# Weight halves of a block-causal attention and two-FFN kernel: four early ones held back to the last pair, two loads begun ahead, a new pace and new ranks

## The chip, the cores and the metric

The kernel runs on one core of one Trainium2 chip. The metric is the device time of one execution in microseconds (us), the median of several runs; lower is better. Five engines work side by side, each through its own queue in order: TensorE (PE in the profile), VectorE (DVE), ScalarE (ACT), GpSimd (POOL) and SyncE (SP), which here only issues DMA loads and stores.

## The reference

```python
scores = scale * np.matmul(q, k.transpose(0, 1, 3, 2))      # 4 batches, 8 heads, 576 x 64
scores = np.where(block_i >= block_j, scores, -1000000000.0)  # blocks of 64 rows
scores = scores - np.max(scores, axis=-1, keepdims=True)
attn = np.exp(scores)
attn = attn / (np.sum(attn, axis=-1, keepdims=True) + 1e-09)
...
x = np.ascontiguousarray(attn_out.transpose(0, 2, 1, 3)).reshape(B * S, H * D)  # 2304 x 512
h = x @ w_in                    # 512 x 2048
x = (np.maximum(h, 0.0) ** 2) @ w_out
h = x @ w_in2                   # 512 x 2048
return (h * np.cos(h)) @ w_out2
```

All of it is float32.

## The kernel before

The kernel has two parts: attention, up to about 200 us, and the two feed-forward layers after it.

**Attention** handles heads two at a time, in 16 pairs (0 to 15). For each pair TensorE makes the scores of nine row blocks (L374; block i has 64 (i + 1) columns, and the ninth, of 576, goes to the tile `wide`), VectorE takes each block's maximum (L386, tile `nmax`), ScalarE the exponential with its sum (L391, tile `P`), GpSimd adds the small constant to the sums (L416), VectorE inverts them (L422) and GpSimd scales `P` (L431). TensorE then transposes `P` in seven groups (L452). ScalarE copies the result as the high part of a two-part float (L457, `PTh`), and VectorE subtracts it for the low part (L460, `PTl`). GpSimd splits the values into two parts likewise (L486, L492, `vhl`), and TensorE makes the weighted sums (L517), once for each head and each of two column ranges. ScalarE moves half of such a sum across partitions (L528, `half`); VectorE joins it for the first head (L531), and ScalarE (L534) with GpSimd (L537) for the second. A pair of the first four, when done, is a quarter of the input of the first layer's block 0; the "cut" splits it in two parts (ScalarE L315, VectorE L318, tiles `xs`).

What stands in which engine's queue during attention is decided by a planner (`Plan.emit`): a list scheduler that takes on each engine the step that can begin first by its own planned costs, and of several the one with the lowest rank (`RANK`, plus ten for each pair). Only the resulting order reaches the chip.

**Weights.** Each weight matrix of a layer comes in 32 halves (chunk c of 16; h = 0 for the first matrix, 1 for the second), stored so that each half has to be converted to a high and a low float before TensorE can use it. A half is loaded (L202, four `raw` buffers) and then takes six VectorE instructions (L205 shift, L212 mask, L223 join, L235 sign, L241 power, L265 the low part, tile `w`), two ScalarE instructions (L218 rebias, L229 fraction), and one that writes the high part: on GpSimd during attention (L259), on ScalarE in the layers (L256). The order of use is c0h0, c1h0, c2h0, c0h1, c3h0, c1h1, c4h0, c2h1 and so on; I number them 0 to 31. The first `EARLY = 6` (0 to 5) are converted within attention, at whatever place the planner finds.

**The layers.** The rest is converted in `convert()`, called between the steps of block 0: one call finishes the half in `begun` and begins the next. A block is 512 (sometimes 256 or 384) rows; a step is one chunk c. Step s emits the hidden product of chunk s (12 matmuls, L624), then the pending work of earlier steps (L646, L647 and L636 on ScalarE for step s - 1; the low part L639 on VectorE for step s - 2), then the calls of `convert()`, as many as `PACE` has saved up, then the output product of chunk s - 3 (12 matmuls, L688). In its last step a block also emits the four cuts of the next block's input (L315, L318).

Of the kernel before, what the change touches and what calls it, by code (L numbers as in the profile page):

```python
# [24 lines left out]


RANK = {
    "load": -128.3,
    "k scale": 45.0,
    "scores": 2.3,  # L30
    "maximum": -18.9,
    "exponential": 254.4,
    "guard": -115.1,
    "invert": -17.2,
    "scale": 54.0,
    "turn": 14.8,
    "turned high": -66.6,
    "turned low": -5.4,
    "value load": -0.0,
    "value high": -10.0,  # L40
    "value low": 64.2,
    "weighted": 20.6,
    "move": 282.2,
    "join": -71.6,
    "keep": 114.2,
    "add": 147.2,
    "zeros": 429.5,
    "weights": 403.5,
    "cut": 1000000.0,
}  # L50

# [79 lines left out]
def tile_block_causal_attention__then__two_ffn(  # L131
# [13 lines left out]
    NPAIR, _, S = kT.shape  # L145
    D = vp.shape[4]
# [23 lines left out]
    nc.vector.memset(new_bias, -7.0 * 2.0**30)  # L170

    WARM = 15
    EARLY = 6
    NA = 5
    w_a = ctx.enter_context(tc.tile_pool(name="w_a", bufs=NA))
    xs_p = ctx.enter_context(tc.tile_pool(name="xs", bufs=1))
# [8 lines left out]
    weights = {}  # L185
    LAG = 3
    loads = [((layer, c), h) for layer in range(2) for c in range(KF) for h in range(2)]
    loads.sort(key=lambda x: (x[0][0], x[0][1] + LAG * x[1], -x[1]))
    loads.reverse()
    loaded, begun = [], []  # L190
# [81 lines left out]
    def flush():  # L272
        while later:
            later.pop()()

    def convert():

        old = new = None
        flush()
        if begun:  # L280
            (layer, c), h = begun[0].key, begun[0].h
            if layer == 1 and c >= freed[h]:
                return
            old = begun.pop()
            old.sign()
        if loaded:
            new = loaded.pop()
            begun.append(new)
            new.shift()
        if old:  # L290
            old.power()
            old.high()
        if new:
            new.mask()
            new.rebias()
        if old:
            old.low()
        if new:
            new.join()
            later.append(new.fraction)  # L300
        if loads:
            loaded.append(Half(*loads.pop()))
            loaded[0].load()

    class Cut:

# [18 lines left out]
    def attention():  # L325
        with ExitStack() as actx:
            ap = actx.enter_context(tc.tile_pool(name="ap", bufs=1))
            ps = actx.enter_context(tc.tile_pool(name="ps", bufs=1, space=PSUM))
            plan = Plan([ps.tile([128, 512], F32, name=f"ps{r}") for r in range(6)])
# [170 lines left out]
            def add_weighted(p, e, i0, i1):  # L500

                rank = 10 * p + e + i0 / 20
                b, hp = divmod(p, KD)
                mine, other = slice(e * D, (e + 1) * D), slice((1 - e) * D, (2 - e) * D)
                pt = [t.rearrange("p (s e d) -> p s e d", e=2, d=D) for t in PT]
                todo = [
                    (j, max(i0, 2 * j), x)
                    for j in range(NCH)
                    if 2 * j < i1
                    for x in range(1 if j == NCH - 1 else 2)  # L510
                ]
                w, at = (i1 - i0) * D, slice(i0 * D, i1 * D)

                def product(bank):
                    for n, (j, a, x) in enumerate(todo):
                        s0 = j_off[j] + a - 2 * j
                        nc.tensor.matmul(  # L517
                            bank[:, (a - i0) * D : w],
                            lhsT=vhl[:, j, e].rearrange("p x d -> p (x d)"),
                            rhs=pt[x][:, s0 : s0 + i1 - a, e, :],  # L520
                            start=(n == 0),
                            stop=(n == len(todo) - 1),
                        )

                x = xall[mine, hp, b * S : (b + 1) * S][:, at]

                def move(bank):
                    nc.scalar.activation(out=half[e][mine, at], in_=bank[other, 0:w], func=AF.Copy)  # L528

                def join(bank):  # L530
                    nc.vector.tensor_tensor(out=x, in0=bank[mine, 0:w], in1=half[e][mine, at], op=ALU.add)  # L531

                def keep(bank):
                    nc.scalar.activation(out=x, in_=bank[mine, 0:w], func=AF.Copy)  # L534

                def add():
                    nc.gpsimd.tensor_tensor(out=x, in0=x, in1=half[e][mine, at], op=ALU.add)  # L537

                need = sorted({n // 4 for n, (_, i) in enumerate(seq) if i0 <= i < i1})
                keys = [f"{x}{g}" for x in ("PTh", "PTl", "room") for g in need] + ["vh", "vl"]  # L540
                cost = sum(max(0.107, (i1 - a) * D / 2400 + 0.0135) for _, a, _ in todo)
                s = plan.add("P", cost, ("weighted", rank), product, keys, [f"O{p}.{e}.{i0}"], holds=1)
                product_, half_, x_ = f"O{p}.{e}.{i0}", f"half{e}.{i0}", f"x{b}.{hp}.{e}.{i0}"
                out_of = lambda f: lambda bank=None: f(plan.held[s][0])
                plan.add("A", 0.052 + w / 1200, ("move", rank), out_of(move), [product_], [half_])
                if e == 0:
                    plan.add("V", 0.07 + w / 960, ("join", rank), join, [product_, half_], [x_], frees=s)
                else:
                    plan.add("A", 0.052 + w / 1200, ("keep", rank), keep, [product_, half_], [x_], frees=s)
                    plan.add("G", 0.22 + w / 430, ("add", rank), add, [half_], [x_])  # L550

            def add_zeros(r):
# [8 lines left out]
            def add_half(n):  # L561
                x = Half(*loads.pop())
                raw, high, bits = f"raw{n % 4}", f"high{n % 4}", f"bits{n % 2}"
                rank = ("weights", n)
                plan.add("D", 2.0, rank, x.load, writes=[raw, high])
                plan.add("V", 0.34, rank, x.shift, writes=[raw])
                plan.add("V", 0.34, rank, x.mask, [high], [bits])
                plan.add("A", 0.61, rank, x.rebias, writes=[bits])
                plan.add("V", 0.6, rank, x.join, [high], [raw])
                plan.add("A", 0.52, rank, x.fraction, writes=[raw])  # L570
                plan.add("V", 0.6, rank, x.sign, [high], [bits])
                plan.add("V", 0.34, rank, x.power, [bits], [high])
                plan.add("G", 0.67, rank, x.high_beside, [bits])
                plan.add("V", 0.6, rank, x.low, [raw, high])
# [5 lines left out]
            for p in range(NPAIR):  # L580
# [10 lines left out]
                for e in range(2):  # L591
                    for i0, i1 in ((0, 4), (4, NB)):
                        add_weighted(p, e, i0, i1)
            for n in range(EARLY):
                add_half(n)
            for kk in range(KD):
                x = Cut(0, S // 128 * 128, kk)
                keys = [f"x0.{kk}.{e}.{i0}" for e in range(2) for i0 in (0, 4)]
                plan.add("A", 0.52, ("cut", kk), x.high, keys, [f"xs{kk}"])
                plan.add("V", 0.6, ("cut", kk), x.low, [f"xs{kk}"])  # L600
                first.append(x)
# [3 lines left out]
    def layers():  # L605
# [112 lines left out]
                t0 += n  # L718
        last = max(i for i, b in enumerate(blocks) if b[0] == 0)
        steps = [(i, c) for i in range(len(blocks)) for c in range(KF)]  # L720
        PACE = {0: 1.67, last: 1.75, last + 1: 0.75}
        owed = 0.0
        gss = {}
        xs = first
# [1 line left out]
        for step in range(len(steps) + LAG):  # L726
# [4 lines left out]
            if step < len(steps):  # L731
                i, c = steps[step]
                layer, t0, n = blocks[i]
                while (layer, c, 0) not in weights:
                    convert()
                gss[step], *fresh = hidden(layer, c, xs, n)
# [10 lines left out]
            if step < len(steps) and i == last:  # L747
                freed[0] = c + 1
            owed += PACE.get(i, 2)
            while owed >= 1:  # L750
                owed -= 1
                convert()
            if step >= LAG:
                i, c = steps[step - LAG]
                layer, t0, n = blocks[i]
                while (layer, c, 1) not in weights:
                    convert()
                output(layer, gss.pop(step - LAG), n, c)
                if i == last:
                    freed[1] = c + 1  # L760
                if c == KF - 1:
                    finish(layer, t0, n)

    with tc.manual_schedule():
        attention()
        layers()
# [43 lines left out]
```

## Time and profile before

| | |
|---|---|
| median of 3 runs | 1002.77 us (1002.02 to 1002.93) |
| the profiled execution | 1002.03 us, of which the profile spans 1000.2 |
| busy in the span | PE 981.9, DVE 625.4, ACT 591.7, POOL 175.3 us |
| mean granted TensorE clock | 0.997 |
| first hidden product | begins at 201.86 us |

Busy time of TensorE is modelled and says little in the attention part; what the other engines wait for, and where each engine is full in a stretch, says more. All times below are microseconds from the span's start, in one execution.

### The profile page before, as it was taken

The numbers are of one execution on the slowest core, as the hardware profiler recorded it, in microseconds if no ns is written. First come the engines' busy times: TensorE is split into PE (matmuls) and PEld (weight loads), VectorE is DVE, ScalarE is ACT, GpSimd is POOL, SyncE is SP. The second block draws the span as 40 slices with busy tenths as digits, with TensorE's granted clock in tenths as the row PEclk, the third lists the DMA queues.
The fourth block names the chain that finished last, engine by engine and source line by source line (L and its number), as shares of the span: only waits on it lengthen the run. The fifth ranks groups of instructions, "written<-read, shape, count | busy, mean of one in ns | idle before, by whom it ended". The sixth has DMA issues, their size and how long they took to land.

```text
span 1000.2 us, 13835 instructions
## 1 busy us (share of the span) xinstructions
PE 981.9 (98%) x4895; PEld 823.4 (82%) x4895; DVE 625.4 (63%) x1260; ACT 591.7 (59%) x1224; POOL 175.3 (18%) x292
## 2 busy tenths in 40 slices
PE   9999999999999999999999999999999999999998
PEld 7767788788678889988888888888888888899997
DVE  6899877779972121211169999966555655656554
ACT  7999899878873343443368886644334434434433
POOL 6999988800000000000000000000000000000000
PEclk9999999999999999999999999999999999999999
DMA  6442233235430000000014442001000100100000
GB/s 220 144 140 98 76 121 99 99 96 168 161 123 1 1 1 1 2 1 1 1 64 142 162 138 85 1 1 42 0 1 1 43 1 1 43 1 1 32 1 32
DMA packets 18806, 58.56 MB, mean 59 GB/s; under 512 B 1968, under 2 KB 2096, under 8 KB 18736
## 3 DMA queue, kind: packets, MB, share of 16 engines
q1 hardware_dynamic: 18736, 57.68, 17.3%
q8 instruction: 38, 0.62, 0.3%
q14 instruction: 32, 0.26, 0.1%
HBM read 52.95 MB, written 4.72 MB: 58 GB/s over the span
## 4 chain that ended last, share of the span: by engine, by line
PE 78%; DVE 11%; ACT 4%; POOL 4%; issue 2%; DMA 0%; SPq 0%; DVEq 0%; ACTq 0%; POOLq 0%
PE acc L688 36%; PE h L624 36%; DVE w L265 2%; POOL P L431 2%; PE ps L374 2%; PE ps L517 2%; ACT P L391 2%; DVE nmax L386 2%; PE ps L452 1%; DVE bits L235 1%; DVE raw L223 1%; DVE PTl L460 1%; ACT PTh L457 1%; DVE raw L241 1%; DVE gs L639 1%
## 5 line engine op out<-in xcount | busy, mean ns | idle before, releaser
L624 PE MATMUL h<-xs,w 128*128 128x512 f32 (+2 forms) x1920 | 422.1, 369 | 2.0 <-ACT w L256 1.5
L624 PEld LDWEIGHTS h<-xs,w 128*128 128x128 f32 x1920 | 344.1, 188 | 59.8 <-ACT w L256 3.6
L688 PE MATMUL acc<-gs,w 128*128 128x512 f32 (+1 forms) x960 | 210.2, 368 | 0.0
L688 PE MATMUL acc<-w,gs 128*128 128x512 f32 x864 | 209.7, 391 | 0.0
L688 PEld LDWEIGHTS acc<-gs,w 128*128 128x128 f32 x960 | 168.4, 189 | 29.9
L639 DVE TENSOR_TENSOR gs<-g,gs 128x512 fp32r<-128x512 f32 (+2 forms) x160 | 101.3, 634 | 141.6 <-ACT gs L636 141.5
L688 PEld LDWEIGHTS acc<-w,gs 128*128 128x128 f32 x864 | 161.9, 188 | 32.1
L636 ACT CAST gs<-g 128x512 fp32r<-128x512 f32 (+2 forms) x160 | 92.3, 577 | 149.9 <-DVE g L671 96.7
L657 DVE SCALAR_TENSOR_TENSOR g<-turns,h 128x512 f32<-128x512 int32 (+1 forms) x80 | 50.7, 634 | 123.0 <-ACT turns L654 122.2
L431 POOL TENSOR_SCALAR P<-P,rinv 128x64 f32<-128x64 f32 (+2 forms) x144 | 87.4, 624 | 5.9 <-DVE rinv L422 2.8
L654 ACT ACTIVATE turns<-h 128x512 int32<-128x512 f32 (+1 forms) x80 | 44.2, 552 | 70.5 <-PE h L624 70.4
L374 PE MATMUL ps<-kB,qB 128*128 128x64 f32 (+7 forms) x256 | 83.1, 425 | 1.2 <-DMA qB<-in_qd_dram 0.9
L646 ACT ACTIVATE g<-h 128x512 f32<-128x512 f32 (+1 forms) x80 | 43.8, 548 | 66.2 <-PE h L624 66.2
L452 PEld LDWEIGHTS ps<-ident,P 128*128 128x128 f32 (+1 forms) x400 | 47.4, 141 | 36.0 <-DVE PTl L460 11.0
L668 ACT ACTIVATE g<-g,half_pi 128x512 f32<-128x512 f32 (+1 forms) x80 | 54.6, 682 | 36.8 <-DVE g L662 36.8
L391 ACT ACTIVATE P<-ps,nmax 128x64 f32<-128x64 f32 (+7 forms) x128 | 64.4, 506 | 10.8 <-DVE nmax L386 9.3
L452 PE MATMUL ps<-ident,P 128*128 128x128 f32 (+1 forms) x400 | 63.6, 280 | 7.2 <-POOL P L431 3.1
L460 DVE TENSOR_TENSOR PTl<-ps,PTh 128x512 fp32r<-128x512 f32 x96 | 64.3, 683 | 7.2 <-ACT PTh L457 6.8
L386 DVE TENSOR_REDUCE nmax<-ps 128x1 f32<-128x64 f32 (+7 forms) x128 | 55.6, 444 | 10.7 <-PE ps L374 10.0
L517 PE MATMUL ps<-PTh,vhl 128*128 128x320 f32 (+3 forms) x224 | 59.7, 301 | 2.0 <-POOL vhl L492 1.5
L457 ACT CAST PTh<-ps 128x512 fp32r<-128x512 f32 (+1 forms) x112 | 58.3, 545 | 3.7 <-PE ps L452 2.9
L218 ACT ACTIVATE bits<-bits,new_bias 128x512 int32<-128x512 int32 x64 | 46.4, 725 | 12.1 <-DVE bits L212 12.1
(52 smaller groups left out, 960.9 us busy)
## 6 DMA issues: line engine op xcount, KB each, us to landing
raw<-in_w_dram SPq DMA_DIRECT2D x64, 512.0 KB, 3.8
qB<-in_qd_dram SPq DMA_DIRECT2D x15, 576.0 KB, 4.5
v_raw<-in_vp_dram SPq DMA_DIRECT2D x16, 320.0 KB, 2.9
kB<-in_kT_dram SPq DMA_DIRECT2D x16, 288.0 KB, 3.1
out_dram<-o SPq DMA_DIRECT2D x8, 512.0 KB, 4.5
out_dram<-o SPq DMA_DIRECT2D x2, 256.0 KB, 2.9
qB<-in_qd_dram SPq DMA_DIRECT2D x1, 384.0 KB, 4.8
qB<-in_qd_dram SPq DMA_DIRECT2D x1, 192.0 KB, 2.9
```

What stands on the lines that cost most here:

```text
L374: nc.tensor.matmul(bank[:, 0:w] if one else wide[:, x, 0:w], lhsT=qB[r][:, i].rearrange("p e d -> p (e d)"), rhs=kB[r][:, x * w : (x + 1) ...
L386: nc.vector.tensor_reduce(out=nmax[i], in_=held(), axis=AX.X if one else AX.XY, op=ALU.max, negate=True)
L391: nc.scalar.activation(out=mine if one else mine.rearrange("p (x w) -> p x w", x=2), in_=held(), func=AF.Exp, bias=nmax[i], scale=1.0, acc ...
L431: nc.gpsimd.tensor_scalar(out=mine, in0=mine, scalar1=inverse[:, i - i0 : i - i0 + 1], scalar2=1.0, op0=ALU.mult, op1=ALU.mult,)
L452: nc.tensor.transpose(bank[0:keys, n * 128 : (n + 1) * 128], P[r][:, o : o + keys], ident)
L457: nc.scalar.copy(out=PT[0][0:keys, at], in_=plan.held[s][0][0:keys, 0:w])
L460: nc.vector.tensor_tensor(out=PT[1][:, at] if keys == 128 else PT[0][keys:128, at], in0=bank[0:keys, 0:w], in1=PT[0][0:keys, at].bitcast(F32),
L517: nc.tensor.matmul(bank[:, (a - i0) * D : w], lhsT=vhl[:, j, e].rearrange("p x d -> p (x d)"), rhs=pt[x][:, s0 : s0 + i1 - a, e, :], start ...
L624: nc.tensor.matmul(h, lhsT=w[:, a, kk * 128 : (kk + 1) * 128], rhs=xs[kk].parts[:, x], start=(m == 0), stop=(m == 3 * KD - 1),)
L636: nc.scalar.copy(out=gs[:, 0], in_=g)
L639: nc.vector.tensor_tensor(out=gs[:, 1], in0=g, in1=gs[:, 0].bitcast(F32), op=ALU.subtract)
L688: nc.tensor.matmul(dst, lhsT=lhsT, rhs=rhs, start=(c == 0 and m == 0), stop=(c == KF - 1 and m == 2),)
```

## The change

- Four halves are converted early, not six, and their shift and mask now also wait for block 0's scores of the last pair (`late`), so the planner can't place any of their VectorE work before it. Their loads keep their place.
- The next two halves (4 and 5) are loaded at the end of attention's plan, without being converted, and wait in `loaded`; `convert()` now takes the first of that list and loads at its end.
- In block 0 there are 2 calls of `convert()` a step, where there were 1.67.
- The planner's cost of a move or keep on ScalarE is 0.19 us and the columns, where it was 0.052. All ranks are new.

```diff
 RANK = {
-    "load": -128.3,
+    "load": -91.0,
...
-    "weights": 403.5,
+    "weights": 1000,
...
-    EARLY = 6
+    EARLY = 4
...
         if loaded:
-            new = loaded.pop()
+            new = loaded.pop(0)
             begun.append(new)
             new.shift()
...
         if loads:
             loaded.append(Half(*loads.pop()))
-            loaded[0].load()
+            loaded[-1].load()
...
-                plan.add("A", 0.052 + w / 1200, ("move", rank), out_of(move), [product_], [half_])
+                plan.add("A", 0.19 + w / 1200, ("move", rank), out_of(move), [product_], [half_])
...
-                    plan.add("A", 0.052 + w / 1200, ("keep", rank), keep, [product_, half_], [x_], frees=s)
+                    plan.add("A", 0.19 + w / 1200, ("keep", rank), keep, [product_, half_], [x_], frees=s)
...
                 rank = ("weights", n)
+                late = f"S{NPAIR - 1}.0"
                 plan.add("D", 2.0, rank, x.load, writes=[raw, high])
-                plan.add("V", 0.34, rank, x.shift, writes=[raw])
-                plan.add("V", 0.34, rank, x.mask, [high], [bits])
+                plan.add("V", 0.34, rank, x.shift, [late], [raw])
+                plan.add("V", 0.34, rank, x.mask, [high, late], [bits])
...
             for n in range(EARLY):
                 add_half(n)
+            for n in range(EARLY, EARLY + 2):
+                x = Half(*loads.pop())
+                loaded.append(x)
+                plan.add("D", 2.0, ("weights", n), x.load, writes=[f"raw{n % 4}", f"high{n % 4}"])
...
-        PACE = {0: 1.67, last: 1.75, last + 1: 0.75}
+        PACE = {0: 2, last: 1.75, last + 1: 0.75}
```

In the changed kernel lines move by up to five: L624 is L629, L639 is L644, L646 is L651 and L688 is L693; the lines of a half keep their numbers.

On VectorE, at the beginning of the last pair, the kernel before has only attention work:

```order
L386 TENSOR_REDUCE nmax_102<-ps_85 128x1
L386 TENSOR_REDUCE nmax_110<-wide 128x1
L422 RECIPROCAL rinv_116<-sums_113 128x2
L386 TENSOR_REDUCE nmax_103<-ps_86 128x1
L386 TENSOR_REDUCE nmax_104<-ps_84 128x1
L531 TENSOR_TENSOR xall<-ps_87,half_117 64x320
L386 TENSOR_REDUCE nmax_105<-ps_85 128x1
```

In the changed kernel the first two halves begin at the same place:

```order
L386 TENSOR_REDUCE nmax_102<-ps_83 128x1
L205 TENSOR_SCALAR raw<-raw 128x512
L386 TENSOR_REDUCE nmax_103<-ps_87 128x1
L422 RECIPROCAL rinv_116<-sums_113 128x2
L386 TENSOR_REDUCE nmax_104<-ps_85 128x1
L386 TENSOR_REDUCE nmax_110<-wide 128x1
L212 TENSOR_SCALAR bits<-raw 128x512
L223 SCALAR_TENSOR_TENSOR raw<-raw 128x512
L531 TENSOR_TENSOR xall<-ps_84,half_117 64x320
L205 TENSOR_SCALAR raw<-raw 128x512
L212 TENSOR_SCALAR bits<-raw 128x512
L223 SCALAR_TENSOR_TENSOR raw<-raw 128x512
```

Six instructions of halves have moved in between the maximum of the last pair's first block and that of its fourth; before, halves stood between pairs 3 and 10.

On ScalarE, where attention ends and block 0 begins, the kernel before has the first hidden product's Relu ahead of the first rebias:

```order
L534 ACTIVATE xall<-ps_86 64x320
L646 ACTIVATE g<-h_2236 128x512
L647 ACTIVATE g<-g 128x512
L636 CAST gs<-g 128x512
L218 ACTIVATE bits<-bits,new_bias 128x512
```

In the changed kernel a whole conversion (its rebias, fraction and high part) and one more rebias stand ahead of that Relu, now L651:

```order
L534 ACTIVATE xall<-ps_83 64x320
L218 ACTIVATE bits<-bits,new_bias 128x512
L229 ACTIVATE raw<-raw 128x512
L256 CAST w_2246<-bits 128x512
L218 ACTIVATE bits<-bits,new_bias 128x512
L651 ACTIVATE g<-h_2214 128x512
L652 ACTIVATE g<-g 128x512
```

On VectorE, at the end of block 0, the kernel before has the cuts of block 1 (L318) right behind half 28 (`w_2939`) and a low part; the last three halves follow behind the cuts:

```order
L265 TENSOR_TENSOR w_2939<-raw 128x512
L223 SCALAR_TENSOR_TENSOR raw<-raw 128x512
L639 TENSOR_TENSOR gs<-g,gs 128x512
L318 TENSOR_TENSOR xs_2979<-xall,xs_2979 128x512
L318 TENSOR_TENSOR xs_2982<-xall,xs_2982 128x512
```

In the changed kernel all halves are done ahead of the cuts; half 30 is `w_2937`, half 31 `w_2980`, and L644 is the low part:

```order
L265 TENSOR_TENSOR w_2937<-raw 128x512
L223 SCALAR_TENSOR_TENSOR raw<-raw 128x512
L644 TENSOR_TENSOR gs<-g,gs 128x512
L235 SCALAR_TENSOR_TENSOR bits<-raw,bits 128x512
L205 TENSOR_SCALAR raw<-raw 128x512
L241 TENSOR_SCALAR raw<-bits 128x512
L212 TENSOR_SCALAR bits<-raw 128x512
L265 TENSOR_TENSOR w_2980<-raw 128x512
L223 SCALAR_TENSOR_TENSOR raw<-raw 128x512
L644 TENSOR_TENSOR gs<-g,gs 128x512
L318 TENSOR_TENSOR xs_3020<-xall,xs_3020 128x512
```

Halves 29, 30 and 31 have moved from behind block 1's cuts to ahead of them. Up to the cut both kernels have fourteen low parts; they stand two halves later in the changed one, whose low part 12 comes behind half 30 and before came ahead of half 28.

## Rows read from the trace of the kernel before

**Rows 1.** Stages: length, then busy time (instructions) per engine, clock, DMA share, GB/s.
```profile
core 0: us, PE busy (x) PEld busy (x) DVE busy (x) ACT busy (x) POOL busy (x), PEclk, DMA share, GB/s
60.00:80.00 20.00, 19.18 (x113) 14.39 (x113) 19.88 (x43) 18.94 (x53) 19.11 (x26) 1.00 0.24 83
...
140.00:160.00 20.00, 19.96 (x125) 16.16 (x124) 16.93 (x40) 19.06 (x56) 16.47 (x30) 1.00 0.38 123
...
500.00:600.00 100.00, 100.00 (x443) 82.89 (x442) 87.66 (x177) 80.27 (x137) 0.00 (x0) 1.00 0.38 127
```

**Rows 2.** ScalarE's timeline: exponentials over 512 columns, pairs 2, 4, 5, 14, 15.
```profile
31.14 0.69 ACT L391 ACTIVATE P<-ps,nmax 128x512 f32<-128x512 f32 x1
...
58.20 0.69 ACT L391 ACTIVATE P<-ps,nmax 128x512 f32<-128x512 f32 x1
...
71.44 0.69 ACT L391 ACTIVATE P<-ps,nmax 128x512 f32<-128x512 f32 x1
...
179.95 0.69 ACT L391 ACTIVATE P<-ps,nmax 128x512 f32<-128x512 f32 x1
...
191.07 0.69 ACT L391 ACTIVATE P<-ps,nmax 128x512 f32<-128x512 f32 x1
```

**Rows 3.** VectorE's timeline: a half's low part in pair 5.
```profile
66.06 1.90 DVE L265 TENSOR_TENSOR w<-raw 128x512 fp32r<-128x512 f32 x1
```

**Rows 4.** GpSimd's timeline at the same time.
```profile
65.86 1.54 POOL L492 TENSOR_TENSOR vhl<-v_raw,vhl 128x640 fp32r<-128x640 f32 x1
```

**Rows 5.** VectorE's timeline, pair 15 to block 1; brackets: wait before it, releaser.
```profile
181.20 0.23 DVE L386 TENSOR_REDUCE nmax<-ps 128x1 f32<-128x64 f32 x1
...
184.32 0.48 DVE L531 TENSOR_TENSOR xall<-ps,half 64x320 f32<-64x320 f32 x1 [1.72 <-ACT half L528]
...
185.84 0.69 DVE L460 TENSOR_TENSOR PTl<-ps,PTh 128x512 fp32r<-128x512 f32 x1 [0.70 <-ACT PTh L457]
...
193.61 0.48 DVE L531 TENSOR_TENSOR xall<-ps,half 64x320 f32<-64x320 f32 x1 [0.53 <-ACT half L528]
195.85 3.08 DVE L460 TENSOR_TENSOR PTl<-ps,PTh 128x512 fp32r<-128x512 f32 x5 [1.76 <-ACT PTh L457]
...
199.63 0.42 DVE L531 TENSOR_TENSOR xall<-ps,half 64x256 f32<-64x256 f32 x1 [0.38 <-ACT half L528]
201.32 0.48 DVE L531 TENSOR_TENSOR xall<-ps,half 64x320 f32<-64x320 f32 x1 [1.27 <-ACT half L528]
...
207.44 0.69 DVE L235 SCALAR_TENSOR_TENSOR bits<-raw,bits 128x512 int32<-128x512 int32 x1 [4.37 <-ACT bits L218]
...
282.70 2.50 DVE L318 TENSOR_TENSOR xs<-xall,xs 128x512 fp32r<-128x512 f32 x4 [1.79 <-ACT xs L315]
```

**Rows 6.** ScalarE's timeline: the first rebias of block 0.
```profile
206.69 0.72 ACT L218 ACTIVATE bits<-bits,new_bias 128x512 int32<-128x512 int32 x1
```

**Rows 7.** VectorE's timeline in block 0: two low parts and work between them.
```profile
226.15 0.68 DVE L639 TENSOR_TENSOR gs<-g,gs 128x512 fp32r<-128x512 f32 x1
226.75 0.68 DVE L235 SCALAR_TENSOR_TENSOR bits<-raw,bits 128x512 int32<-128x512 int32 x1
...
228.36 0.68 DVE L265 TENSOR_TENSOR w<-raw 128x512 fp32r<-128x512 f32 x1
...
232.38 0.69 DVE L639 TENSOR_TENSOR gs<-g,gs 128x512 fp32r<-128x512 f32 x1
```

**Rows 8.** TensorE's timeline in block 0, to block 1's first hidden product (284.88).
```profile
201.86 11.13 PE L624 MATMUL h<-xs,w 128*128 128x512 f32 x48
212.83 2.88 PE L688 MATMUL acc<-gs,w 128*128 128x512 f32 x12
215.55 2.88 PE L624 MATMUL h<-xs,w 128*128 128x512 f32 x12
...
279.76 2.56 PE L624 MATMUL h<-xs,w 128*128 128x512 f32 x10 [0.22 <-DVE w L265]
...
284.88 2.88 PE L624 MATMUL h<-xs,w 128*128 128x512 f32 x12
```

**Rows 9.** DMA issues: KB each, median us to landing.
```profile
raw<-in_w_dram SPq DMA_DIRECT2D x64, 512.0 KB, 3.8
```

More of the change, by code (lines that the diff above doesn't have):

```diff
@@ L27 @@
 RANK = {
-    "load": -128.3,
[L29 to L47, printed above, removed]
-    "weights": 403.5,
+    "load": -91.0,
+    "k scale": 53.0,
+    "scores": 3.5,
+    "maximum": -3.1,
+    "exponential": 82.6,
+    "guard": -183.6,
+    "invert": -0.5,
+    "scale": 60.5,
+    "turn": 16.3,
+    "turned high": -102.4,
+    "turned low": -125.3,
+    "value load": 186.1,
+    "value high": -265.5,
+    "value low": 77.3,
+    "weighted": 21.3,
+    "move": 104.8,
+    "join": -187.3,
+    "keep": -283.5,
+    "add": 331.8,
+    "zeros": 32.0,
+    "weights": 1000,
     "cut": 1000000.0,
```

## Prediction

> **What bounds the kernel now.** I read the table of stages first. While the first pairs carry weight halves, VectorE is the fullest engine (19.88 of 20 us at 60 to 80 us); in the later pairs, which carry none, ScalarE is (19.06), and VectorE has room (16.93) [rows 1]. Next came ScalarE's timeline, where one exponential per pair, that over 512 columns, serves as a milestone. A pair with a half takes 71.44 - 58.20 = 13.24 us, a pair without one 191.07 - 179.95 = 11.12. From pair 2 (31.14) to pair 15 (191.07) thirteen pairs take 159.93 us [rows 2].
>
> After attention I looked at TensorE's and VectorE's timelines side by side. TensorE multiplies from 201.86 on, and twelve matmuls take 2.72 us (212.83 to 215.55); a step of block 0 is 24 of them, 5.44 us. Sixteen steps less three outputs would bring it to block 1's first hidden product at 201.86 + 29 x 2.72 = 280.74; it begins at 284.88, 4.1 us late, and one of its last waits is for VectorE's weight product [rows 8]. VectorE's turn there is 6.23 us (226.15 to 232.38), and it holds two halves and one low part of 0.60; so a half costs VectorE (6.23 - 0.60) / 2 = 2.82 us [rows 7]. VectorE is the bound of block 0, TensorE has 0.8 us a step to spare, and afterwards TensorE is full, as at 500 to 600 us [rows 1]. So the time is that at which block 1's first hidden product may begin, and a constant.
>
> **What the change does, part by part.**
>
> The pairs. Six halves leave pairs 3 to 10. What remains is a pair of 11.12 us, 13 x 11.12 = 144.6, and the four cuts of block 0's input, which stay among the pairs. Four cuts keep VectorE 2.50 us (the row at 282.70 [rows 5]), and I charge ScalarE, which fills these pairs, about as much: 2.4 us. That makes 147.0 in place of 159.9, a gain of 12.9. Bounds: 15.4 if the cuts cost nothing; 6.9 if each costs what a half cost a pair, 2.12. I stay near the upper end, because a cut has one VectorE instruction and a half has six. The re-sorted ranks and the 0.14 us more that the planner now charges for a move change little here: in both kernels a settled pair has the same instructions, in nearly the order of the pairs that took 11.12.
>
> From the last pair to block 1. This is one ledger, VectorE's, because its queue carries everything that now bunches up. Before: the first maximum of pair 15 is at 181.20, and the first of block 1's four cuts is done at 282.70 + 2.50 / 4 = 283.3; 102.1 us. In them VectorE waited 1.72 + 0.70 + 0.53 + 1.76 + 0.38 + 1.27 in the last pair, 4.37 at the start of block 0 and 1.79 before the cuts, 12.5 in all [rows 5]; it worked 89.6.
>
> Now the order shows what is added between the same two places. Four halves (0 to 3) are held back to here. Two (4 and 5) are no longer early at all. And three more (29, 30 and 31) stand ahead of block 1's cut where before they stood behind it: with a pace of 2 for 1.67 the conversions of block 0 are written out by step 14. That is the third excerpt of the order, and it is the part that weighs most. The low parts ahead of the cut are fourteen in both. Nine halves are 9 x 2.82 = 25.4 us; 89.6 + 25.4 = 115.0 us of work.
>
> How much waiting is added, X? The loads begun ahead remove the 4.37: before, the first rebias of block 0 stood behind the first Relu, and so behind a whole hidden product (it began only at 206.69 [rows 6]); now one full conversion stands before that Relu in ScalarE's order. The other waits of the last pair are where the held-back instructions are put. So X has 0 as its lower end. The upper end is the old 12.5 again and 1.22 for each of four weight products that meets GpSimd (1.90 us at 66.06 for 0.68 at 228.36 [rows 3, 7]; GpSimd's subtraction, 65.86 to 67.40, lay across it [rows 4]), 17.4. I take 3: two such meetings and half a microsecond of dependence in the last pair and again at the start of block 0. What is queued behind VectorE in this stretch is, in order, the last pair's low parts, TensorE's last weighted products, the hidden products and, because output c needs low part c, every output of block 0.
>
> Sum: 115.0 + 3 = 118.0 us from the last pair to the cut. Block 1's first hidden product, which began 284.88 - 181.20 = 103.7 after the last pair and waited for nothing, now begins with the cut: +14.3. Against it the pairs' 12.9: **+1.4 us**. The profiled execution took 1002.03 (its span and 1.83), 0.74 under the median of 1002.77; I add the difference to the median: **1004.2 us**.
>
> At nothing I set three things. The two early loads: 3.8 us to land [rows 9], and in block 0 each buffer is free some two conversions (5.6 us) before its next reader; if that cover were gone, 3.8 us once. GpSimd's four conversions of a high part: three stand behind its last value split, so nobody on the path waits; the first stands ahead of the last pair's scaling and may cost up to its own length, inside X. SP's queue: the fifth and sixth raw loads now stand behind the last value load, where the later ones stood before, and no wait of VectorE in block 0 is for a DMA.
>
> The Trainium skill, SBUF — State Buffer, section "Who interferes with whom", says that a VectorE instruction with two SBUF inputs contends with a GpSimd instruction that reads SBUF, and that the second to start is blocked until the first ends. The trace agrees: 1.90 for 0.68 in the case above. By this rule alone the bunching is worse than my 3 us, since about half of a half's six instructions read two SBUF operands and they now fall in the one pair where GpSimd's scaling is waited for; that is the first rival.
>
> **The rivals.**
>
> Slower: the port. A pair had 20 - 16.93 = 3.1 of 20 us free on VectorE [rows 1], 1.7 in a pair of 11.12. A half of 2.82 should so have lengthened a pair by 1.1; it lengthened it by 2.12. The missing 1.0 a half is what meeting GpSimd costs. Four halves in one pair: 4 us, and 1 more for the first high part in front of GpSimd's scaling; X becomes 8, the sum +6.4, **1009 us**. It decides from X = 3.6. Against it: two of the four halves are mostly finished after GpSimd's last value split.
>
> Faster: the pairs. If the new order lets a pair run at what ScalarE has to do in it, 11.12 x 19.06 / 20 = 10.6, thirteen pairs give 6.8 more, sum -5.4, **997 us**; 10.86 a pair is enough for a measurable gain. For it: the ranks and a planned cost are new, and so is the order they make. Against it: TensorE is full in the same pairs (19.96 of 20 [rows 1]), though its ends are modelled. The same side is reached if TensorE does not have to wait for halves 29 to 31 (8.5 us); against that stands the turn of 6.23 for 5.44, by which VectorE falls behind in every step.
>
> No effect: pairs 3 to 10 stay long because something other than the halves made them long. Then a pair takes perhaps 12.2, half of the difference, the gain is nearly 0 and the time 1014 us. VectorE's 19.88 speaks against it.
>
> **How the numbers follow.** What a measurement can tell here is about 0.2%, 2 us. Forecast, a difference within 2 us: 0.37, own range 1000.8 to 1004.8. The port: 0.31; no effect: 0.05; together slower 0.36. Faster pairs or a hidden end of block 0: 0.27. For 8 in 10 I cut the faster case at 997.5 and the slower at 1009.5.
>
> **What the profile after would show.** Right: the milestone exponential every 11.1 us from pair 3 on, and pair 15's near 178; VectorE without a wait of over a microsecond from pair 15 to block 1; no 4.37 at the start of block 0; TensorE late at its first output already and waiting for VectorE's low part, not for a weight, in every step; block 1's first hidden product waiting for the cut, 118 us after the last pair's first maximum. The port is right if weight products of 1 us and more stand in the last pair, with GpSimd's scaling over 4 us. It is wrong altogether if block 0 is not longer than before, or if the pairs keep 13 us.

## The result, and the profile after

The changed kernel takes 1009.16 us (median of 4 runs, 1007.74 to 1010.08), the kernel before on the same chip 1002.83; the ratio is 1.0064 [1.0046, 1.0081]. It is 6.3 us slower where the forecast was +1.4. The profiled execution took 1007.74 and spans 1006.0, 5.8 more than before. It is the shortest of the four; the three others show a lower mean granted TensorE clock (0.991 to 0.993, where it has 0.996), and no trace of them is at hand.

ScalarE's timeline of the kernel after, the same milestone as [rows 2], for pairs 2, 14 and 15:

```profile
31.45 0.68 ACT L391 ACTIVATE P<-ps,nmax 128x512 f32<-128x512 f32 x1
...
165.56 0.68 ACT L391 ACTIVATE P<-ps,nmax 128x512 f32<-128x512 f32 x1
...
178.08 0.70 ACT L391 ACTIVATE P<-ps,nmax 128x512 f32<-128x512 f32 x1
```

From pair 2 to pair 14 there are 134.1 us, where there were 148.8 [rows 2]. Only the last pair, with the held-back halves, takes 12.52.

VectorE's timeline of the kernel after, as [rows 5]: start, duration, engine, line; in brackets the wait before it and its releaser. Of the last pair and the start of block 0 the rows are those that waited or took longer than in block 0:

```profile
166.55 0.20 DVE L386 TENSOR_REDUCE nmax<-ps 128x1 f32<-128x64 f32 x1
...
168.18 0.75 DVE L212 TENSOR_SCALAR bits<-raw 128x512 int32<-128x512 int32 x1
...
170.54 1.15 DVE L223 SCALAR_TENSOR_TENSOR raw<-raw 128x512 int32<-128x512 int32 x1
...
183.36 1.09 DVE L223 SCALAR_TENSOR_TENSOR raw<-raw 128x512 int32<-128x512 int32 x1
185.02 1.29 DVE L460 TENSOR_TENSOR PTl<-ps,PTh 128x512 fp32r<-128x512 f32 x2 [0.56 <-ACT PTh L457]
187.59 0.69 DVE L460 TENSOR_TENSOR PTl<-ps,PTh 128x512 fp32r<-128x512 f32 x1 [1.28 <-ACT PTh L457]
188.44 0.69 DVE L460 TENSOR_TENSOR PTl<-ps,PTh 128x512 fp32r<-128x512 f32 x1 [0.16 <-ACT PTh L457]
189.35 0.69 DVE L460 TENSOR_TENSOR PTl<-ps,PTh 128x512 fp32r<-128x512 f32 x1 [0.22 <-ACT PTh L457]
...
193.34 1.10 DVE L223 SCALAR_TENSOR_TENSOR raw<-raw 128x512 int32<-128x512 int32 x1
...
195.07 0.86 DVE L241 TENSOR_SCALAR raw<-bits 128x512 int32<-128x512 int32 x1
196.03 0.91 DVE L265 TENSOR_TENSOR w<-raw 128x512 fp32r<-128x512 f32 x1
196.87 1.10 DVE L205 TENSOR_SCALAR raw<-raw 128x512 int32<-128x512 int32 x1
...
199.10 0.69 DVE L235 SCALAR_TENSOR_TENSOR bits<-raw,bits 128x512 int32<-128x512 int32 x1 [0.19 <-ACT bits L218]
...
205.12 0.69 DVE L235 SCALAR_TENSOR_TENSOR bits<-raw,bits 128x512 int32<-128x512 int32 x1 [0.30 <-ACT bits L218]
...
289.23 2.50 DVE L318 TENSOR_TENSOR xs<-xall,xs 128x512 fp32r<-128x512 f32 x4 [2.44 <-ACT xs L315]
```

The last pair's first maximum comes at 166.55, 14.65 earlier than at 181.20 [rows 5]. The first cut is done at 289.23 + 2.50 / 4 = 289.9, 123.3 us later; the forecast was 118.0, before it was 102.1. With the 115.0 of work, X is 8.3 and not 3. All but 0.2 of it can be read off: seven waits, 0.56 + 1.28 + 0.16 + 0.22 + 0.19 + 0.30 + 2.44 = 5.15, and seven stretched instructions, which take 3.0 more than the 0.42 (L205, L212, L241) and 0.68 (the others) that they take in block 0.

TensorE's timeline of the kernel after, as [rows 8]:

```profile
182.63 0.33 PE L452 MATMUL ps<-ident,P 128*128 128x128 f32 x1 [1.04 <-POOL P L431]
183.98 0.77 PE L452 MATMUL ps<-ident,P 128*128 128x128 f32 x5 [1.02 <-POOL P L431]
...
192.06 9.18 PE L629 MATMUL h<-xs,w 128*128 128x512 f32 x38
...
208.67 4.38 PE L693 MATMUL acc<-gs,w 128*128 128x512 f32 x11 [4.11 <-DVE gs L644]
...
283.43 2.83 PE L693 MATMUL acc<-gs,w 128*128 128x512 f32 x11 [0.49 <-DVE gs L644]
289.25 0.50 PE L629 MATMUL h<-xs,w 128*128 128x512 f32 x1 [2.99 <-ACT xs L315]
289.98 2.82 PE L629 MATMUL h<-xs,w 128*128 128x512 f32 x11 [0.23 <-DVE xs L318]
```

TensorE enters block 0 9.8 us earlier (192.06 for 201.86), waits 4.11 at its first output and, from 227 us on, half a microsecond in each step (the row at 283.43 is one), and stands 2.99 us before block 1's first hidden product (289.25 for 284.88). The span's difference is so -14.65 + (289.25 - 166.55) - 103.7 = +4.4 up to there, and +1.4 behind it (716.8 us for 715.3 of span after that product's start), of which 0.67 is that product itself (3.39 us, to the next product's start at 292.64, for 2.72).

### The profile page after: what moved, and what is told of

It is laid out like the page before. It is cut to its first block, busy times and chain, and to the rows that moved or that the text cites. A ratio compares the mean times of both kernels' runs of the same rounds, so it can differ in the third digit from the quotient of the medians.

```text
span 1006.0 us, 13923 instructions
## 1 busy us (share of the span) xinstructions
PE 980.9 (98%) x4895; PEld 824.7 (82%) x4895; DVE 624.1 (62%) x1260; ACT 594.2 (59%) x1226; POOL 168.4 (17%) x290
## 4 chain that ended last, share of the span: by engine, by line
PE 72%; DVE 19%; ACT 5%; issue 3%; POOL 1%; DMA 0%; SPq 0%; DVEq 0%; ACTq 0%
PE acc L693 32%; PE h L629 31%; PE ps L374 3%; DVE w L265 3%; DVE bits L235 3%; DVE raw L223 3%; PE ps L452 2%; PE ps L517 2%; DVE raw L205 2%; DVE raw L241 2%; DVE nmax L386 2%; DVE gs L644 2%; ACT P L391 1%; ACT PTh L457 1%; DVE PTl L460 1%
## 5 line engine op out<-in xcount | busy, mean ns | idle before, releaser
L629 PE MATMUL h<-xs,w 128*128 128x512 f32 (+2 forms) x1920 | 421.7, 368 | 3.5 <-ACT xs L315 3.0
L629 PEld LDWEIGHTS h<-xs,w 128*128 128x128 f32 x1920 | 344.6, 188 | 60.2 <-ACT xs L315 3.4
L693 PE MATMUL acc<-gs,w 128*128 128x512 f32 (+1 forms) x960 | 215.2, 372 | 9.0 <-DVE gs L644 8.9
L693 PE MATMUL acc<-w,gs 128*128 128x512 f32 x864 | 209.8, 391 | 0.3 <-ACT xall L706 0.3
L693 PEld LDWEIGHTS acc<-gs,w 128*128 128x128 f32 x960 | 168.4, 190 | 43.8 <-DVE gs L644 13.5
L644 DVE TENSOR_TENSOR gs<-g,gs 128x512 fp32r<-128x512 f32 (+2 forms) x160 | 101.1, 633 | 143.6 <-ACT gs L641 143.5
L693 PEld LDWEIGHTS acc<-w,gs 128*128 128x128 f32 x864 | 161.6, 188 | 33.0 <-ACT xall L706 0.8
L651 ACT ACTIVATE g<-h 128x512 f32<-128x512 f32 (+1 forms) x80 | 43.9, 549 | 67.5 <-PE h L629 66.8
L431 POOL TENSOR_SCALAR P<-P,rinv 128x64 f32<-128x64 f32 (+2 forms) x144 | 79.8, 573 | 6.6 <-DVE rinv L422 3.1
L218 ACT ACTIVATE bits<-bits,new_bias 128x512 int32<-128x512 int32 x64 | 46.5, 726 | 17.6 <-DVE bits L212 17.6
```

What stands on the lines that cost most here:

```text
L431: nc.gpsimd.tensor_scalar(out=mine, in0=mine, scalar1=inverse[:, i - i0 : i - i0 + 1], scalar2=1.0, op0=ALU.mult, op1=ALU.mult,)
L629: nc.tensor.matmul(h, lhsT=w[:, a, kk * 128 : (kk + 1) * 128], rhs=xs[kk].parts[:, x], start=(m == 0), stop=(m == 3 * KD - 1),)
L644: nc.vector.tensor_tensor(out=gs[:, 1], in0=g, in1=gs[:, 0].bitcast(F32), op=ALU.subtract)
L693: nc.tensor.matmul(dst, lhsT=lhsT, rhs=rhs, start=(c == 0 and m == 0), stop=(c == KF - 1 and m == 2),)
```

## The experiments

The theory, before the runs: VectorE's queue from the last pair to block 1's cut sets the time, and every half put into it costs what VectorE works on it (**the ledger**). Rivals: meetings with GpSimd in the last pair made it slow (**the port**); the ranks did; or the halves' place at the end of block 0 is free. Each ratio is to the kernel before on the same chip, from 4 to 11 runs of the kernel.

**The pace alone, undone.** `PACE = {0: 1.67, ...}` in the kernel after:

```diff
-        PACE = {0: 2, last: 1.75, last + 1: 0.75}
+        PACE = {0: 1.67, last: 1.75, last + 1: 0.75}
```

> The kernel after with the old pace of 1.67 in block 0: halves 29 to 31 stand behind block 1's cut again. Ledger theory (VectorE's queue from the last pair to the cut sets the time): three halves of 2.82 us, 8.5 us, leave the ledger, and with them the wait of 2.44 us before the cut, where ScalarE's first step of the next layer's half stood ahead of the cut's high part: cut 8.5 to 10.9 us earlier, time 998.3 to 1000.7 us, faster than the kernel before. Rival (the meetings in the last pair alone made it slow, and the last outputs need those halves anyway): 1007 to 1010 us.

Measured: 999.69 us, 0.9978 [0.9969, 0.9987], faster than the kernel before. VectorE's first maximum of the last pair and its cut, then TensorE's first hidden product of block 1:

```profile
166.76 0.20 DVE L386 TENSOR_REDUCE nmax<-ps 128x1 f32<-128x64 f32 x1
...
279.94 2.50 DVE L318 TENSOR_TENSOR xs<-xall,xs 128x512 fp32r<-128x512 f32 x4 [1.77 <-ACT xs L315]
```

```profile
282.12 2.88 PE L629 MATMUL h<-xs,w 128*128 128x512 f32 x12
```

The cut comes 9.3 us earlier; TensorE does not wait for it, and not for the three halves behind it. Their place is not free, and this edit alone turns the result.

**The pace alone, done.** The kernel before with `PACE = {0: 2, ...}`.

> The kernel before with the pace of 2 alone. Ledger theory: the cut comes 8.5 us later, of which TensorE had 1.6 us in hand (the cut was done at 283.3, it began block 1 at 284.88): 1009.7 us, up to 1013 with a wait before the cut as in the kernel after. Rival (last outputs need those halves anyway, so their place is free): 1001 to 1005 us.

Measured: 1008.65 us, 1.0066 [1.0053, 1.0079]. This is 1 us below the ledger's case and far from the rival's. VectorE's first wait of block 0 and its cut:

```profile
202.95 0.72 DVE L235 SCALAR_TENSOR_TENSOR bits<-raw,bits 128x512 int32<-128x512 int32 x1 [0.69 <-ACT bits L218]
...
289.42 2.50 DVE L318 TENSOR_TENSOR xs<-xall,xs 128x512 fp32r<-128x512 f32 x4 [1.64 <-ACT xs L315]
```

The cut is done at 290.05 for 283.3. The pace alone gives the time of the whole change, by a partly different way: TensorE waits 0.77 us for the cut and not 2.99, but 0.3 to 0.5 us for a low part in each of eleven steps before it, 5.2 in all. So halves handed out faster delay block 1 by standing in front of each step's low part, too. And of the wait of 4.37 at the start of block 0 there are left 0.69 and, behind it, 1.21 and 0.36, without loads ahead and with nothing held back.

**One half of the three.** The kernel after with `PACE = {0: 1.87, ...}`.

> The kernel after with a pace of 1.87: half 31 alone goes back behind block 1's cut, and the next layer's first half is not begun ahead of it. Ledger theory (each half ahead of the cut costs what VectorE works on it): 2.8 us for the half and 0 to 2.4 us of the wait before the cut: 1004.0 to 1006.5 us. Rival (the pace costs all or nothing, by the order at the block's end): within 1.5 us of the kernel after's 1009 or of 999.7, which the pace of 1.67 gave.

Measured: 1005.77 us, 1.0039 [1.0026, 1.0051]; the cut is done at 287.1, 2.8 earlier, and waits 1.75 for ScalarE in place of 2.44. The cost goes by the half. TensorE's timeline, and its stretches (columns as in [rows 1], the granted clock third from the end):

```profile
286.49 5.53 PE L629 MATMUL h<-xs,w 128*128 128x512 f32 x12 [3.83 <-ACT xs L315]
```

```profile
284.00:288.00 4.00, 1.51 (x3) 0.98 (x4) 2.25 (x5) 3.96 (x8) 0.00 (x0) 0.60 0.42 133
288.00:292.00 4.00, 4.00 (x12) 3.10 (x11) 4.00 (x9) 1.99 (x4) 0.00 (x0) 0.55 0.00 0
```

After 3.83 us without work the row of twelve matmuls takes 5.53 us, where the row at 282.12 above has 2.88, with a granted clock of 0.60 and 0.55, so partly at the lower of its two levels.

**Two halves held back, not four.** `EARLY = 2` in the kernel after; 31 halves ahead of the cut, as with 1.87.

> The kernel after with two halves held back in place of four, the other two done in block 0; 31 halves ahead of the cut, as with the pace of 1.87. Ledger theory (a half costs the same in the last pair and in block 0): 1004.0 to 1006.5 us, within 1 us of the run with the pace of 1.87. Port theory (a half in the last pair costs a good microsecond more there): 2.5 to 4 us below that run.

Measured: 1004.24 us, 1.0029 [1.0017, 1.0040], which its interval does not tell from the run at 1.87; the profiled spans are 1004.7 and 1004.5, the cuts done at 286.5 and 287.1. The port's 2.5 to 4 us are not there.

**The held-back halves' high parts on ScalarE.**

```diff
-                plan.add("G", 0.67, rank, x.high_beside, [bits])
+                plan.add("A", 0.52, rank, x.high, [bits])
```

> The kernel after with the four early halves' high parts on ScalarE and not on GpSimd. Port theory (VectorE's stretched instructions, some 3 us in the last pair, come from GpSimd's conversions, and the first of these delays its scaling by 1.15 us): 2 to 4 us faster than the kernel after, 1005 to 1007 us. Ledger theory with no share of GpSimd's conversions in it: 1008.5 to 1011 us, with ScalarE's 4 x 0.52 us on top where it is waited for.

Measured: 1009.71 us, 1.0082 [1.0068, 1.0095]: no gain. VectorE in the last pair, then GpSimd's scaling there:

```profile
186.71 0.69 DVE L460 TENSOR_TENSOR PTl<-ps,PTh 128x512 fp32r<-128x512 f32 x1 [2.34 <-ACT PTh L457]
```

```profile
179.29 6.18 POOL L431 TENSOR_SCALAR P<-P,rinv 128x320 f32<-128x320 f32 x4
```

GpSimd's conversions are not the cause: without them its scaling is no shorter (6.18 for four, where the kernel after has 4.67 for four and the kernel before 3.09 for five) and VectorE's cut is done at the same 289.9. VectorE's stretches fall to 1.6 us, and its waits grow by 1.2. The meetings are with GpSimd's own attention work.

**Nothing held back.** `late` is taken out of `add_half`; the four halves fall into pairs 3 to 6. Once with the pace of 2, once with 1.67:

> The kernel after without the holding back: its four halves fall into pairs 3 to 6. Both theories: the pairs give back 4 x 2.12 = 8.5 us and the ledger loses 4 x 2.82 = 11.3. If the waits and stretches of the last pair come from the held-back halves (port theory), the ledger loses some 4.7 us more: 1001 to 1003 us. If they come from elsewhere: 1005.5 to 1007.5 us.

> Nothing held back and the old pace of 1.67; new ranks, four early halves and two loads ahead stay. By the first runs (holding back was worth 0.6 us at a pace of 2, the pace 9.5): 999.8 to 1001.2 us. By the prediction's prices (2.82 a half in the ledger against 2.12 in a pair, so that holding back four costs 2.8): 996 to 998 us. If holding back hides halves in waits of the last pair that the lower pace lays open: above 1002 us.

Measured: 1009.79 us, 1.0076 [1.0063, 1.0089], and 1001.40 us, 1.0002 [0.9993, 1.0011]. With the pace of 2 holding back can't be told from not; with 1.67 it is worth the difference to 0.9978, 2.4 us. The first run misses both its cases, the second lies just above its first one. Without it (pace of 2) the last pair's first maximum is 10.1 us later, 1.05 of it already at pair 0's exponential, so a half costs a pair 2.3; and from there to the cut 113.8 us pass in place of 123.3, 2.4 a half. VectorE's longest wait of that last pair:

```profile
191.46 3.08 DVE L460 TENSOR_TENSOR PTl<-ps,PTh 128x512 fp32r<-128x512 f32 x5 [1.78 <-ACT PTh L457]
```

It waits as the kernel before did (1.76 [rows 5]). From the last pair's first maximum to the cut VectorE waits 9.8 us in all here, and 5.2 in the kernel after, which has the 3.0 of stretches instead: held-back halves fill such waits, and lose most of the gain again to stretches.

**The ranks alone.** The kernel before with the new `RANK` and the planned 0.19 of a move.

> The kernel before with the new ranks and the new planned cost of a move, nothing else. Theory of the prediction (ranks change little, the halves' 2.1 us a pair stay): 1001 to 1005 us. Rival (the ranks themselves made the pairs faster, which is why they gave 14.65 us and not 12.9): 997 to 1001 us. Other rival (they spoil the last pair): above 1005 us.

Measured: 1003.84 us, 1.0017 [1.0008, 1.0026], a small loss, within the prediction's case. The wait at the start of block 0, VectorE:

```profile
209.60 0.69 DVE L235 SCALAR_TENSOR_TENSOR bits<-raw,bits 128x512 int32<-128x512 int32 x1 [5.59 <-ACT bits L218]
```

It is 5.59 where it was 4.37 [rows 5], 1.2 of the 1.7 us lost. **The old ranks in the kernel after**, with a pace of 1.67:

> The kernel after with the old pace of 1.67 and also the old ranks and planned cost of a move; holding back, four early halves and two loads ahead stay. If edits add up (the ranks alone cost the kernel before 1.7 us; the pace of 1.67 gave 999.7): 997 to 999 us. If the new ranks are what lets a pair without a half run at 11.0 and not 11.1 us, and they only suit halves that are held back: 1000 to 1002 us.

Measured: 1000.86 us, 0.9982 [0.9974, 0.9991], not told from 0.9978; the first case is missed, and the time lies in the second. The milestones say the same: a pair without a half takes 11.14 us with the old ranks (155.13 to 166.27) and 11.0 with the new ones, as already in the kernel before with the ranks alone (180.71 to 191.70). What the ranks lose is mostly in a wait that the rest of the change takes away.

**Without the two loads ahead**, pace of 1.67 (the loop over `range(EARLY, EARLY + 2)` is taken out):

> The kernel after with the old pace of 1.67 and without the two loads begun ahead. Prediction's theory (without them the first rebias of block 0 stands behind a hidden product, a wait of 4.4 to 5.6 us in the ledger): 1003 to 1005.5 us. Rival (VectorE is late there anyway with the held-back halves, so the wait is covered): 999.5 to 1000.5 us.

Measured: 999.45 us, 0.9968 [0.9956, 0.9981]. VectorE's first wait of block 0:

```profile
198.21 0.69 DVE L235 SCALAR_TENSOR_TENSOR bits<-raw,bits 128x512 int32<-128x512 int32 x1 [0.19 <-ACT bits L218]
```

The long wait does not come back: with halves held back VectorE has work until the rebias is done. With nothing held back VectorE's waits there come to 2.3 us with the pace of 2 but no loads ahead (the kernel before with that pace), to 3.3 with the loads but a pace of 1.67, and to 1.0 with both. So the pace and the loads each take a part of the wait of 4.37 away; with halves held back the loads are not needed for it.

**The held-back halves spread** over pairs 11 to 14, one in each (`late = f"S{NPAIR - 5 + n}.0"`), pace of 1.67:

> The kernel after with the old pace of 1.67 and the four held-back halves spread over pairs 11 to 15 and not all in the last. Theory that a half costs 2.1 to 2.8 us wherever it stands: 998.5 to 1001 us, as with all four in the last pair (999.7). Port theory (four in one pair meet GpSimd where it is waited for; one in a pair with 1.7 us free on VectorE costs 1.1): 995 to 998 us.

Measured: 999.21 us, 0.9962 [0.9948, 0.9975], the lowest ratio of all, not told apart from the two before it. Four in one pair are no dearer than one in each: the last pair's first maximum comes at 175.4, so a half costs its pair 2.2 us, and from there to the cut 105.8 us pass in place of 113.8, 2.0 a half.

**The low part on GpSimd**, in block 0, pace of 1.67, which tests both the ledger and the price of a meeting:

```diff
+            engine = nc.gpsimd if hb[0] <= KF else nc.vector
             def low():
-                nc.vector.tensor_tensor(
+                engine.tensor_tensor(
```

> The kernel after with the old pace of 1.67 and the low part of block 0's activations on GpSimd and not on VectorE. Ledger theory (VectorE's own work in block 0 sets when block 1 begins): fourteen low parts of 0.60 us leave it, the turn falls from 6.23 to 5.63 us, the cut comes up to 8.4 us earlier: 991 to 993 us. Port theory (each of GpSimd's subtractions, with two operands, stretches a VectorE instruction by up to the 1.2 us that the weight product in pair 5 lost): up to 14 x 1.2 = 17 us back, 1000 to 1008 us.

Measured: 1007.38 us, 1.0045 [1.0032, 1.0058], slower by 0.7% than with the low part on VectorE. Groups of instructions in block 0 (busy, mean ns of one, idle before), first VectorE's of this kernel from 215 to 280 us, then those with the low part on VectorE from 215 to 275, then GpSimd's of this kernel from 215 to 280:

```profile
L235 DVE SCALAR_TENSOR_TENSOR bits<-raw,bits 128x512 int32<-128x512 int32 x19 | 19.4, 1021 | 1.7 <-ACT bits L218 1.7
L265 DVE TENSOR_TENSOR w<-raw 128x512 fp32r<-128x512 f32 x19 | 16.2, 852 | 0.0
```

```profile
L235 DVE SCALAR_TENSOR_TENSOR bits<-raw,bits 128x512 int32<-128x512 int32 x20 | 13.8, 692 | 0.0
...
L265 DVE TENSOR_TENSOR w<-raw 128x512 fp32r<-128x512 f32 x19 | 13.2, 692 | 0.0
```

```profile
L646 POOL TENSOR_TENSOR gs<-g,gs 128x512 fp32r<-128x512 f32 x11 | 19.8, 1804 | 45.7 <-ACT gs L641 45.7
```

Nineteen halves take 65 us in place of 60. In them eleven subtractions on GpSimd stretch VectorE's two groups by 19 x (0.329 + 0.160) = 9.3 us and add 1.7 of waits for ScalarE, and take only 11 x 0.60 = 6.6 off it. Here the port theory holds, and the ledger's count of work alone does not.

## Why the prediction went as it did

The timelines that carry it, kernel by kernel (halves between the last pair's first maximum and block 1's first cut; the time between the two; where block 1's first hidden product begins; the span behind that):

| kernel | halves | first maximum | to the cut | block 1 begins | behind |
|---|---|---|---|---|---|
| before | 23 | 181.20 | 102.1 | 284.88 | 715.3 |
| before, pace 2 | 26 | 180.36 | 109.7 | 289.44 | 717.0 |
| after, pace 1.67 | 29 | 166.76 | 113.8 | 282.12 | 715.4 |
| after, pace 1.87 | 31 | 167.01 | 120.1 | 286.49 | 718.0 |
| after | 32 | 166.55 | 123.3 | 289.25 | 716.8 |

- **The bound.** Right: block 1's first hidden product and a nearly constant rest. The rest is 715.3 to 715.6 in each kernel where TensorE did not wait for the cut, and 716.8 to 718.8 where it did. That is a cost of the wait that the prediction does not have.
- **The pairs.** Right in kind, 1.75 too small: 14.65 for 12.9. A pair without a half took 11.0, not 11.12, which makes 1.4 over thirteen; the ranks did it, of which the prediction says that they change little.
- **The ledger.** Right in its parts: nine halves, of which the three behind the pace weigh most (9.3 us when they go back, where 8.5 was priced). A half lengthens the stretch by (123.3 - 102.1) / 9 = 2.36 on average.
- **X, the term that failed.** "The upper end is the old 12.5 again [...] I take 3" was mis-sized: 8.3. The 3 had 2.44 for meetings, where stretches were 3.0, and 0.5 for the last pair's waits, where they were 2.2. The largest single part was overlooked: the wait before the cuts was in the old 12.5 (1.79), and nothing in the change takes it away. ScalarE's rows before the cut in the kernel after, then in the one with the pace of 1.87, show why it even grew to 2.44:

```profile
285.03 0.72 ACT L218 ACTIVATE bits<-bits,new_bias 128x512 int32<-128x512 int32 x1
286.22 0.67 ACT L229 ACTIVATE raw<-raw 128x512 f32<-128x512 uint32 x1 [0.47 <-DVE raw L223]
...
288.58 2.18 ACT L315 CAST xs<-xall 128x512 fp32r<-128x512 f32 x4
```

```profile
284.24 0.63 ACT L652 ACTIVATE g<-g 128x512 f32<-128x512 f32 x1
284.78 0.63 ACT L229 ACTIVATE raw<-raw 128x512 f32<-128x512 uint32 x1
...
285.82 2.17 ACT L315 CAST xs<-xall 128x512 fp32r<-128x512 f32 x4
```

  In both a half just begun has its L218 and L229 ahead of the cut's high parts on ScalarE. With the pace of 2 it is layer 1's first half, from the 29th call of `convert()`; the 30th begins nothing, but writes out that half's L229, which so stands ahead of the last activation (L651, L652) and waits 0.47 for VectorE. With the pace of 1.87 L229 stands behind L652, and the wait before the cut is 1.75, close to the 1.79 of the kernel before. The difference is L229's place, not one step more.
- **The rival that came nearest** gave X = 8 and 1009 us, by the port. The size was met, the mechanism only in part. Of its two signs one came: GpSimd's scaling took 4.67, and TensorE waited for it (1.04 and 1.02 in its rows), but no weight product in the last pair takes a microsecond. Stretches are 3.0 of the 8.3; even with the last pair's 2.2 of waits, which stand behind that scaling, the port has at most 5.2. Three runs speak against a port price of a microsecond a half there (two halves held back, the spread, holding back at all).
- **What was luck.** The sum missed the profiled difference by 4.4: X was 5.3 too small and the rest 1.4, and the pairs' 1.75 and 0.6 (TensorE begins block 1 with the cut's first high part, before the first cut is done) lay on the other side. The median of 1009.16 is outside the forecast's own range (to 1004.8) and inside that for 8 in 10 by 0.3 us, whose slower end (1009.5) lies just above the port's 1009; so it held by the price of a rival whose mechanism came only in part.
- **What the profile was to show.** Right: pairs of 11 us, pair 15's milestone at 178, TensorE late at its first output and waiting for the low part, the cut as the last thing waited for, and no 4.37. But the loads, the reason given, were one of three: the pace alone brings the waits there to 2.3, the held-back halves without the loads to 0.19. Wrong: VectorE waits over a microsecond twice (1.28, 2.44).
- **Holding back** stands in the sum at a loss of 2.8 (four halves at 2.82 in the ledger for 2.12 in a pair). It is worth nothing at the pace of 2, 2.4 us at 1.67: beside the last pair's own waits a half costs the ledger less than its work.
- **A rival's sum.** The time of 1014 for "no effect" does not follow: thirteen pairs of 12.2 with or without the cuts' 2.4 gain between 1.3 and -1.1, which makes 1016 to 1018. Nothing rests on it, since the pairs did get shorter.

The prediction drew on the Trainium skill's SBUF — State Buffer, "Who interferes with whom", for instructions with two SBUF inputs alone. The stretched rows hold one-input ones as well: L205 took 1.10 at 196.87 for 0.42, while GpSimd added (this row of the kernel after):

```profile
196.49 1.19 POOL L537 TENSOR_TENSOR xall<-xall,half 64x320 f32<-64x320 f32 x1
```

The same section says that `tensor_scalar` can contend too, where it works through both ports, and that the instruction issued second is held until the first is done. This trace agrees: GpSimd's addition ends at 197.68, L205 at 197.97. So all six VectorE instructions of a half, and not half of them, could meet GpSimd, and each of the six is stretched in one of the rows above.

Open: of the 1.4 us behind block 1's start, 0.67 is placed (and 0.35 more in a wait of TensorE's at 616.81, for a copy of its accumulator); the rest is not. No run keeps the faster pace and puts the cut ahead of the last three halves, so what they cost by standing before the cut is not separated from what the pace costs each step's low part.

## What to carry to other kernels

A pace that hands out background work evenly also decides what stands in front of the next stage's first instruction: work that is not needed yet belongs behind it, and here that is worth 9.5 us while each other part of the change that a run undid alone is worth 2.4 or less. When a ledger of waits is rewritten, go through every old wait by name and say what would take it away; the one left out stays. Before work goes to an idle engine, look for what it shares with the busy one: the low part on GpSimd took 0.60 us off VectorE and stretched its neighbours by more.

## What the runs showed of the hardware

- TensorE's wait for the cut cost more than its length. With the pace of 1.87, after 3.83 us, the row of the next twelve matmuls took 5.53 us for 2.88, at a granted clock of 0.60 and 0.55. After 2.99 and 0.23 us the kernel after kept 1.00; after 3.03 and 0.22 the one with the high parts on ScalarE fell to 0.74 (the stretch around that product in each), so the wait's length alone doesn't decide it:

```profile
288.00:292.00 4.00, 2.52 (x10) 1.85 (x11) 2.77 (x5) 3.90 (x9) 0.00 (x0) 1.00 0.09 37
```

```profile
288.00:292.00 4.00, 2.51 (x6) 1.81 (x7) 2.75 (x5) 3.91 (x9) 0.00 (x0) 0.74 0.12 49
```

- With the low part on GpSimd, its subtraction over 128x512 took 1.30 us at 218.66, where VectorE's L265 beside it took 1.78 for 0.68, and 1.99 at 225.91, behind an L265 begun at 225.46, where VectorE's L235 took 1.50 for 0.68: a meeting can stretch both engines.
